# Attention on one Trainium2 core: the eleven phases of a unit get a table of their own

## The chip, the cores and the metric

The kernel runs on one core of one Trainium2 chip. The metric is device time in microseconds (us) of one execution. A profiled execution of the same program gives the start and the duration of every instruction; its own time stands in the table below.

## The reference

Four layers follow each other on one sequence of S = 2048 tokens with D = 576 features. Layers 0 and 2 are attention with H = 32 heads of Dh = 18 features ("A"); layers 1 and 3 have 32 query heads and one head of keys and values ("B").

```python
x = x + _A_ref(_layernorm(x), A_wqkv, A_wo)
x = x + _B_ref(_layernorm(x), B_wq, B_wk, B_wv, B_wo)
x = x + _A_ref(_layernorm(x), A_wqkv, A_wo)
x = x + _B_ref(_layernorm(x), B_wq, B_wk, B_wv, B_wo)
# in each _ref, per head:
scores = einsum("bhqd,bhkd->bhqk", q, k) * Dh ** -0.5
o = einsum("bhqk,bhkd->bhqd", softmax(scores), v)      # then all heads @ wo
```

All is in float32.

## The kernel before

**Units.** Two heads form a pair p; four blocks u of 512 queries form the sequence. One (p, u) is a unit: 64 units in a layer, 256 in the program. A row vector of q or k is held in three parts (54 rows) with a few more rows for the maximum; head a = 0 lies in partitions 0 to 63, head a = 1 in partitions 64 to 127. So a row product uses one half of the TensorE array, and two of them, one on each half, can run side by side.

**What a unit does.** The scores are computed twice. The first time, for the maximum over the keys: 32 row products of 62 rows and 512 columns (`max_mm`, L506, "m" below). Two of them fill the two banks of a tile `psm`, and one VectorE reduction (L515) takes both, so a unit has 16 reductions. There are two `psm` tiles, so the third pair can begin when the first has been reduced. After the last pair of a unit `max_final` (L625) reduces the 32 partial maxima to 8 columns of negated maxima, two small GpSimd operations split them, VectorE transposes them (L634), and DMAs put them into two rows of q. The maxima run 28 pairs, that is 1.75 units, ahead of the rest. The second time, the maximum is subtracted in the product itself: 32 row products of 64 rows and 512 columns (`exp_mm`, L649, "e" below), each into one of three banks `pse`, each followed by a ScalarE exponential (L653) into an SBUF tile `pt`. Then the value products (`pv_block`, L674): four `pt` tiles at a time are multiplied with the values, on four column groups of 32 columns of the array side by side, and accumulated in the one bank `oacc`; ones beside the values give the sums of the softmax. A block has 512 columns, a unit eight blocks, 4096 columns. At the end of a unit ScalarE copies `oacc` (L680), and GpSimd and DMAs do the division.

**The order of the work.** Every engine works through its instructions in the order of the program. The loop over `phase` writes that order out: eleven phases make a unit, numbered 0 to 10 here. A phase is a run of row products, followed by a number of value columns, two phases behind. Before the change `ORDERS` has three kinds of phase: even phases (0, 2, 4, 6, 8) have five row products, odd ones seven, and phase 10 has four. In all phases the halves alternate. With two rows of different halves side by side a phase of five takes three slots of time, one of seven takes four, and phase 10 two: 5 x 3 + 5 x 4 + 2 = 37 slots, of which ten hold a single row, each the last of its phase. A phase has 384 value columns, phase 10 has 256. The maxima's heads are the `n ^ k // 2 % 2` of the loop. `run_todo` issues the small steps and DMAs of finished units at the beginning of the phases, by the number of exponentials issued so far.

The rest of a layer (projections, layer norm, the output projection) is not touched.

Of the kernel before, what the change touches and what calls it, by code (L numbers as in the profile page):

```python
# [19 lines left out]
NCH = S // P  # L20
NPAIR = H // 2
# [21 lines left out]
STEPS = 8  # L43
LEAD = 14
# [14 lines left out]

ORDERS = ([("m", 1), ("e", 0), ("m", 1), ("e", 1), ("e", 2)],
          [("m", 0), ("m", 1), ("e", 1), ("e", 0), ("m", 0), ("m", 1), ("e", 2)],
          [("m", 1), ("e", 0), ("m", 1), ("e", 1)])


@with_exitstack
def tile_kernel(ctx: ExitStack, tc: tile.TileContext, A_x, A_wqkv, A_wo, B_x, B_wq, B_wk, B_wv, B_wo, out):
# [53 lines left out]
    def mtile2(name):  # L123
        return psum.tile([P, 2, 512], F32, tag="m", bufs=2, name=name)
# [7 lines left out]
    def ptile(name, shape=(P, 512), dt=F32):  # L132
        return pool.tile(list(shape), dt, tag="p", bufs=15, name=name)
# [200 lines left out]
    def out_proj(last):  # L334

        for c in range(NCH):
            tt = c // 2
            if c == 1:
                out_rows(2)
            if c % 2 and tt + 3 < 8:  # L340
                out_rows(tt + 3)
            if c >= OUT_AHEAD:
                run_tail(TAIL)
            out_w(c)
            if c % 2 == 0 and tt + 1 < 8:
                out_t(tt + 1, nc.scalar)
            if last:
                nc.sync.dma_start(y_out[c * P:(c + 1) * P, :], xo[:, c])
            yield c
        assert not tail and not ors  # L350
# [4 lines left out]
    for layer in range(4):  # L355
# [124 lines left out]
        def ops(p):  # L480
            return big[:, q_slot(p)], big[:, k_slot(p)]

        m_open, m_next, m_done, m_count = [], [0, 0], [0], {}

        m_first = [] if is_a else ([(0, i // 2, i % 2) for i in range(8)] + [(1, i // 2, i % 2) for i in range(4)] +
                                   [(0, i, 2) for i in range(4)] + [(1, i // 2, i % 2) for i in range(4, 6)] +
                                   [(0, i, 3) for i in range(4)] + [(1, i // 2, i % 2) for i in range(6, 8)] +
                                   [(1, i, 2) for i in range(4)] + [(1, i, 3) for i in range(4)])

        def max_mm(a, slot):  # L490

            i = m_next[a]
            p, u = divmod(i // 16, 4)
            if i < len(m_first):
                u, qc, kb = m_first[i]
            else:
                qc, kb = i // 2 % 4, i // 8 % 2 * 2 + i % 2
            q, k = ops(p)
            if (p, u) not in mxs:
                mxs[p, u] = pool.tile([P, 32], F32, name="mx")  # L500
            if m_done[0] % 2 == 0:
                m_open.append((mtile2("psm"), []))
            ps, rows = m_open[0]
            b = 64 * a
            c0 = u * 512 + qc * P
            nc.tensor.matmul(ps[:, slot], q[b:b + KM, c0:c0 + P], k[b:b + KM, kb * 512:(kb + 1) * 512],  # L506
                             start=True, stop=True)
            rows.append((p, u, 16 * a + 4 * qc + kb))
            m_next[a] += 1
            m_done[0] += 1  # L510
            if m_done[0] % 2 == 0:
                m_open.pop()
                (p, u, r0), (p1, u1, r1) = sorted(rows)
                assert (p, u) == (p1, u1)
                nc.vector.reduce_max(mxs[p, u][:, r0:r1 + 1:r1 - r0], ps, axis=AX.X)  # L515
                m_count[p, u] = m_count.get((p, u), 0) + 2
                if m_count[p, u] == 32:
                    max_final(p, u)

        def max_pair():  # L520
            if is_a and m_done[0] % 4 == 0:
                run_todo(m_done[0] // 4)
            for a in range(2):
                max_mm(a, a)
            if not is_a and m_done[0] == 46:
                max_store(0, 0)
            elif not is_a and m_done[0] == 54:
                max_rows(0, 0)
# [94 lines left out]
        def max_final(p, u):  # L623
            neg = pool.tile([P, 8], F32, name="neg")
            nc.vector.tensor_reduce(neg, mxs.pop((p, u)).rearrange("p (b k) -> p b k", k=4), axis=AX.X, op=OP.max,  # L625
                                    negate=True)
            hl = nms[p, u] = hls[(4 * p + u) % 2]
            copy(nc.gpsimd, hl[:, 0:8], neg)
            nc.gpsimd.tensor_tensor(hl[:, 8:16], neg, hl.bitcast(F32)[:, 0:8], op=OP.subtract)

        def max_store(p, u):

            tr = pool.tile([P, 32], F32, name="tr")
            nc.vector.transpose(tr, nms.pop((p, u)).bitcast(F32))  # L634
            for b in range(4):
                nc.sync.dma_start(m_d[u].rearrange("j a q (b i) -> b (j a q) i", b=4)[b], tr[32 * b:32 * b + 16, :])

        def max_rows(p, u):
            for a in range(2):
                nc.sync.dma_start(big_f[64 * a + KM:64 * a + KE, q_slot(p), u * 512:(u + 1) * 512],  # L640
                                  m_d[u][:, a].rearrange("j q p -> j (q p)"))

        def exp_mm(p, u, i, tail):

            a, kc = (i // 2) % 2, i // 4 * 2 + i % 2
            q, k = ops(p)
            e = (mtile if tail and i % 2 else etile)("pse")
            r = 64 * a
            nc.tensor.matmul(e, k[r:r + KE, kc * P:(kc + 1) * P], q[r:r + KE, u * 512:(u + 1) * 512],  # L649
                             start=True, stop=True)  # L650

            pt = pts[p, u, i] = ptile("pt")
            nc.scalar.activation(pt, e, AF.Exp, scale=SCALE)  # L653
# [3 lines left out]
        def pv_cols(cols):  # L657

            while cols:
                n, c0 = divmod(pv_at[0], 512)  # L660
                w = min(cols, 512 - c0)
                pv_block(n, c0, c0 + w)
                pv_at[0] += w
                cols -= w

        def pv_block(n, c0, c1):

            p, u, i = *divmod(n // STEPS, 4), n % STEPS * 4
            cs = slice(c0, c1)
            turn[0] += 1  # L670
            for i in range(i, i + 4) if turn[0] % 2 else range(i + 3, i - 1, -1):
                a, kc = (i // 2) % 2, i // 4 * 2 + i % 2
                j = 64 * a + 32 * (kc % 2)
                nc.tensor.matmul(oacc[j:j + DH + 1, cs], v_of(kc)[:, 2 * p + a if is_a else 0, :], pts[p, u, i][:, cs],  # L674
                                 start=kc < 2 and c0 == 0, stop=kc >= 14 and c1 == 512)
                if c1 == 512:
                    pts.pop((p, u, i))
            if c1 == 512 and i // 4 == STEPS - 1:
                oc = ocs[p, u] = ptile("oc")
                nc.scalar.activation(oc, oacc, AF.Copy)  # L680
# [38 lines left out]
        def at(b, f, *args):  # L719
            todo.setdefault(b, []).append((f, args))  # L720

        ns = STEPS * 4 * NPAIR
        for p in range(NPAIR):
            for u in range(4):
                b = STEPS * (4 * p + u) + STEPS - 1
# [20 lines left out]
        def run_todo(st):  # L746
            for n in sorted(n for n in todo if n <= st):
                for f, args in todo.pop(n):
                    f(*args)
# [4 lines left out]
        at(b - 1, out_rows, 1)  # L754
        left = 2 * LEAD - m_done[0] // 2
        woven(max_pair, left, len(fill) * len(TERMS) // left)
        for f, args in fill:
            f(*args)
        assert not weave["left"]
        exps = 0  # L760
        for phase in range(11 * 4 * NPAIR):
            k = phase % 11
            run_todo(LEAD + exps // 4)
            for kind, n in ORDERS[2 if k == 10 else k % 2]:
                if kind == "e":
                    n += exps
                    exp_mm(*divmod(n // 4 // STEPS, 4), n % (4 * STEPS), m_done[0] >= 4 * ns)
                elif m_done[0] < 4 * ns:
                    max_mm(n ^ k // 2 % 2, m_done[0] % 2 if k % 2 == 0 else n ^ k // 2 % 2)
            exps += 2 if k == 10 else 3  # L770
            if phase >= 2:
                pv_cols(256 if k == 10 else 384)
        outs = out_proj(layer == 3)
        for st in range(ns, ns + L_AT + 1):
            run_todo(LEAD + st)
            if st < ns + OUT_AHEAD:
                next(outs)
                pv_cols(256 * (1 + st - ns))
        tail = [todo.pop(n, []) for n in range(ns + LEAD + L_AT + 1, ns + LEAD + O_AT)]
        assert not todo, todo  # L780

# [30 lines left out]
```

## Time and profile before

| | |
|---|---|
| median of 3 runs | 5818.13 us (5813.65 to 5818.87) |
| profiled execution, its own time | 5815.04 us |
| its span, first to last instruction | 5813.3 us |
| TensorE matmuls, busy | 5783.1 us (99%) |
| VectorE, busy | 5173.7 us (89%) |
| ScalarE, busy | 4604.9 us (79%) |
| GpSimd, busy | 1714.7 us (29%) |
| row products for the exponentials (L649) | 8192, 2450.5 us |
| row products for the maxima (L506) | 8192, 2296.7 us |
| granted TensorE clock | 0.998 |

In the profile PE is TensorE's matmuls and PEld its weight loads, DVE is VectorE, ACT ScalarE, POOL GpSimd, SP the engine that issues the DMAs. Busy times are sums over overlapping work: a busy PE is not a PE at its peak, since matmuls of two halves or of four column groups run at once. A line of a timeline has the start, the time to the end of the last merged instruction, the engine, line and tile, the number of merged instructions, and in brackets the idle time before it and what ended it.

### The profile page before, as it was taken

The page shows a single profiled execution, that of the slowest core. Times are in us where ns is not written, and L with a number is a line of the kernel's source. Part 1 is how long each engine was busy: PE and PEld are TensorE (multiplying, and loading weights), DVE is VectorE, ACT ScalarE, POOL GpSimd, SP SyncE. Part 2 cuts the span into 40 slices and gives each one's busy share as a digit, 9 for nine tenths or more (in the row PEclk, how much of TensorE's full clock was granted, in tenths as well). Part 3 has the DMA queues.
Part 4 walks back from the last instruction along what each step waited for, and adds up shares of the span by engine and source line. Part 5 has one row for each costly group of instructions (what it writes and reads, how often), then busy time and mean ns, then how long its engine had stood idle before and what let it go on. Part 6 is the DMA issues. An engine that isn't in the chain of part 4 may idle for free.

```text
span 5813.3 us, 132695 instructions
## 1 busy us (share of the span) xinstructions
PE 5783.1 (99%) x53756; PEld 2903.9 (50%) x53756; DVE 5173.7 (89%) x5336; ACT 4604.9 (79%) x8872; POOL 1714.7 (29%) x2207
## 2 busy tenths in 40 slices
PE   9999999999999999999999999999999999999999
PEld 7644444444844444444685444444448444444446
DVE  4799999998699999999637999999976999999995
ACT  2588888888378888888625888888882888888885
POOL 2132322223233232323311323232342332323232
PEclk9999999999999999999999999999999999999999
DMA  5311111110320000000243111111114100000002
GB/s 199 105 44 32 35 32 34 33 32 22 126 65 23 23 20 22 20 22 23 59 167 89 42 35 31 35 31 35 29 32 129 51 22 23 22 23 19 23 14 77
DMA packets 250305, 276.40 MB, mean 48 GB/s; under 512 B 131732, under 2 KB 171924, under 8 KB 239972
## 3 DMA queue, kind: packets, MB, share of 16 engines
q1 hardware_dynamic: 249692, 267.92, 16.6%
q8 instruction: 422, 6.91, 0.5%
q14 instruction: 191, 1.56, 0.1%
HBM read 151.24 MB, written 112.56 MB: 45 GB/s over the span
## 4 chain that ended last, share of the span: by engine, by line
PE 97%; DVE 1%; DMA 0%; POOL 0%; ACT 0%; issue 0%; SPq 0%; POOLq 0%; ACTq 0%; DVEq 0%
PE oacc L674 36%; PE psm L506 31%; PE pse L649 17%; PE psn L215 6%; PE psq L374 6%; DVE mx L515 1%; PE ps L207 0%; DMA raw<-in_B_wk_dram 0%; ACT pt L653 0%; PE oacc L208 0%; SPq L151 0%; POOL big L162 0%; DMA raw<-in_A_wqkv_dram 0%; DVE xh L255 0%; DVE st L244 0%
## 5 line engine op out<-in xcount | busy, mean ns | idle before, releaser
L515 DVE TENSOR_REDUCE mx<-psm 128x2 f32<-128x1024 f32 x4096 | 4771.9, 1217 | 172.8 <-PE psm L506 130.6
L653 ACT ACTIVATE pt<-pse 128x512 f32<-128x512 f32 x8192 | 4315.4, 603 | 543.7 <-PE pse L649 376.3
L649 PE MATMUL pse<-big 64*128 64x512 f32 x8192 | 2450.5, 417 | 3.1 <-ACT evr L385 1.8
L506 PE MATMUL psm<-big 62*128 62x512 f32 x8192 | 2296.7, 453 | 6.8 <-DVE mx L515 6.5
L674 PE MATMUL oacc<-pt,vbuf 128*19 128x384 f32 (+1 forms) x24560 | 1757.1, 385 | 1.9 <-ACT oc L680 1.9
L506 PEld LDWEIGHTS psm<-big 62*128 62x128 f32 x8192 | 926.5, 184 | 1480.1 <-DVE mx L515 926.9
L649 PEld LDWEIGHTS pse<-big 64*128 64x128 f32 x8192 | 1188.6, 185 | 286.4 <-ACT pt L653 192.8
L674 PEld LDWEIGHTS oacc<-pt,vbuf 128*19 128x19 f32 x24560 | 500.9, 97 | 773.2 <-issue 595.7
L139 POOL TENSOR_SCALAR hl<-neg 128x8 fp32r<-128x8 f32 x256 | 50.6, 198 | 2669.7 <-DVE neg L625 2669.7
L674 PE MATMUL oacc<-pt,vy 128*19 128x256 f32 x8176 | 592.0, 384 | 0.0
L697 POOL TENSOR_TENSOR rl<-lt,mone 128x8 f32<-128x8 f32 x256 | 422.5, 1651 | 572.2 <-DMA lt<-os 572.1
L139 POOL TENSOR_SCALAR os<-oc 32x512 f32<-32x512 f32 x512 | 313.3, 612 | 130.8 <-ACT oc L680 88.7
L710 POOL TENSOR_TENSOR os<-os,rb 96x512 f32<-96x512 f32 x256 | 328.3, 1282 | 21.1 <-DMA rb<-r_d 20.3
L688 POOL TENSOR_TENSOR os<-os,oc 96x512 f32<-96x512 f32 x256 | 326.2, 1274 | 21.3
L382 ACT ACTIVATE ev<-psq 128x512 fp32r<-128x512 f32 (+1 forms) x112 | 66.9, 597 | 329.2 <-PE psq L374 229.9
L215 PE MATMUL psn<-wsm,xx 128*128 128x288 f32 x2240 | 313.3, 297 | 0.0
L215 PEld LDWEIGHTS psn<-wsm,xx 128*128 128x128 f32 x2240 | 299.3, 188 | 15.9 <-issue 15.6
L674 PEld LDWEIGHTS oacc<-pt,vy 128*19 128x19 f32 x8176 | 177.0, 98 | 249.6 <-issue 200.6
L388 DVE TENSOR_TENSOR ev<-psq,ev 128x512 fp32r<-128x512 f32 (+1 forms) x84 | 58.0, 690 | 217.4 <-ACT ev L382 201.7
L374 PE MATMUL psq<-yx,big 128*128 128x512 f32 (+2 forms) x812 | 200.2, 397 | 2.1 <-ACT big L137 0.8
L374 PE MATMUL psq<-xx,big 128*128 128x512 f32 (+1 forms) x784 | 201.0, 401 | 0.0
L680 ACT ACTIVATE oc<-oacc 128x512 f32<-128x512 f32 x256 | 158.2, 618 | 28.2 <-PE oacc L674 28.2
(66 smaller groups left out, 1367.2 us busy)
## 6 DMA issues: line engine op xcount, KB each, us to landing
big<-qk_d SPq DMA_DIRECT2D x180, 432.0 KB
qk_d<-ev SPq DMA_DIRECT2D x96, 512.0 KB
qk_d<-ev SPq DMA_DIRECT2D x120, 256.0 KB
rb<-r_d SPq DMA_DIRECT2D x512, 36.0 KB
o_d<-os SPq DMA_DIRECT2D x512, 36.0 KB
m_d<-tr SPq DMA_DIRECT2D x1024, 2.0 KB
o<-o_d SPq DMA_DIRECT2D x64, 256.0 KB
big<-m_d SPq DMA_DIRECT2D x512, 4.0 KB
```

What stands on the lines that cost most here:

```text
L139: eng.tensor_scalar(dst, src, 1.0, 0.0, op0=OP.mult, op1=OP.add)
L215: nc.tensor.matmul(ps, lhs[:, xc, :], wsm[:, wc, h * 288:(h + 1) * 288], start=i == 0, stop=i == len(TERMS) - 1)
L374: nc.tensor.matmul(ps[:n].rearrange("p (u t) -> p u t", u=2)[:, us], w[:, wc, :n], xts[T][:, us, xc, :], start=j == 0, stop=j == len(TERMS ...
L506: nc.tensor.matmul(ps[:, slot], q[b:b + KM, c0:c0 + P], k[b:b + KM, kb * 512:(kb + 1) * 512], start=True, stop=True)
L515: nc.vector.reduce_max(mxs[p, u][:, r0:r1 + 1:r1 - r0], ps, axis=AX.X)
L649: nc.tensor.matmul(e, k[r:r + KE, kc * P:(kc + 1) * P], q[r:r + KE, u * 512:(u + 1) * 512], start=True, stop=True)
L653: nc.scalar.activation(pt, e, AF.Exp, scale=SCALE)
L674: nc.tensor.matmul(oacc[j:j + DH + 1, cs], v_of(kc)[:, 2 * p + a if is_a else 0, :], pts[p, u, i][:, cs], start=kc < 2 and c0 == 0, stop=k ...
L680: nc.scalar.activation(oc, oacc, AF.Copy)
L688: nc.gpsimd.tensor_tensor(t[:96], t[:96], oc[:96], op=OP.add)
L697: nc.gpsimd.tensor_tensor(rl, lts.pop((p, u)), mone, op=OP.pow)
L710: nc.gpsimd.tensor_tensor(t[:96], t[:96], rb[:96], op=OP.mult)
```

## The change

Each of the eleven phases gets an entry of its own in a table: the order of its row products (m or e, with the head) and its number of value columns. The exponentials are now taken head by head (`e_next`), the maxima in the order of the table; `m_heads` lists the heads of all maxima in advance, and `m_banks` tells for each pair which of the two goes to which bank of `psm`, so that the reduction's output can be written in rising order.

```diff
-ORDERS = ([("m", 1), ("e", 0), ("m", 1), ("e", 1), ("e", 2)],
-          [("m", 0), ("m", 1), ("e", 1), ("e", 0), ("m", 0), ("m", 1), ("e", 2)],
-          [("m", 1), ("e", 0), ("m", 1), ("e", 1)])
+UNIT = [("m1 m0 e0 e0 e1 m0 m1", 352), ("e1 m0 e1 m1 e0", 384), ("m0 m1 e1 e1 e0 m1 m0", 384), ("e0 m1 m0 e0 e1", 384),
+        ("m1 e0 e1 m0 e0 m1", 352), ("m0 e1 e0 m1 e1 m0", 416), ("e0 e1 m0 m0 e1", 192), ("e0 m1 e1 m0", 320),
+        ("m0 m1 e0 e0 e1 m0 m1", 384), ("e1 e0 m1 m1 e0", 352), ("m0 m1 e1 e1 e0 m1 m0", 576)]
+UNIT = [([(o[0], int(o[1])) for o in rows.split()], cols) for rows, cols in UNIT]
...
-        def max_mm(a, slot):
+        def max_place(a, i):
...
+        m_heads = ([0, 1] * (2 * LEAD) + [g for rows, _ in UNIT for kind, g in rows if kind == "m"] * (4 * NPAIR))[:4 * ns]
+        m_banks, n = [], [0, 0]
+        for i in range(0, 4 * ns, 2):
+            at_ = []
+            for a in m_heads[i:i + 2]:
+                p, u, qc, kb = max_place(a, n[a])
+                at_.append((p, u, 16 * a + 4 * qc + kb))
+                n[a] += 1
+            m_banks += [0, 1] if at_[0] < at_[1] else [1, 0]
+
+        def max_mm():
+
+            a, slot = m_heads[m_done[0]], m_banks[m_done[0]]
+            p, u, qc, kb = max_place(a, m_next[a])
...
-        exps = 0
-        for phase in range(11 * 4 * NPAIR):
-            k = phase % 11
-            run_todo(LEAD + exps // 4)
-            for kind, n in ORDERS[2 if k == 10 else k % 2]:
+        e_next = [0, 0]
+        for phase in range(len(UNIT) * 4 * NPAIR):
+            rows, cols = UNIT[phase % len(UNIT)]
+            run_todo(LEAD + sum(e_next) // 4)
+            for kind, a in rows:
                 if kind == "e":
-                    n += exps
-                    exp_mm(*divmod(n // 4 // STEPS, 4), n % (4 * STEPS), m_done[0] >= 4 * ns)
+                    pu, kc = divmod(e_next[a], NCH)
+                    exp_mm(*divmod(pu, 4), kc // 2 * 4 + 2 * a + kc % 2, m_done[0] >= 4 * ns)
+                    e_next[a] += 1
                 elif m_done[0] < 4 * ns:
-                    max_mm(n ^ k // 2 % 2, m_done[0] % 2 if k % 2 == 0 else n ^ k // 2 % 2)
-            exps += 2 if k == 10 else 3
+                    max_mm()
             if phase >= 2:
-                pv_cols(256 if k == 10 else 384)
+                pv_cols(cols)
...
-                pv_cols(256 * (1 + st - ns))
+                pv_cols(512 if st > ns else UNIT[0][1] + UNIT[1][1] - 512)
```

Per unit there are still 32 row products of each kind, 4096 value columns in eleven runs, and 16 stretches of columns into which the block boundaries cut them. Phases 0, 2, 8 and 10 now have seven rows, 1, 3, 6 and 9 five, 4 and 5 six, and phase 7 four.

More of the change, by code (lines that the diff above doesn't have):

```diff
@@ L488, in tile_kernel @@
                                    [(1, i, 2) for i in range(4)] + [(1, i, 3) for i in range(4)])
-        def max_mm(a, slot):
-            i = m_next[a]
+        def max_place(a, i):
             p, u = divmod(i // 16, 4)
             if i < len(m_first):
-                u, qc, kb = m_first[i]
-            else:
-                qc, kb = i // 2 % 4, i // 8 % 2 * 2 + i % 2
+                return (0, *m_first[i])
+            return p, u, i // 2 % 4, i // 8 % 2 * 2 + i % 2
+        ns = STEPS * 4 * NPAIR
+        m_heads = ([0, 1] * (2 * LEAD) + [g for rows, _ in UNIT for kind, g in rows if kind == "m"] * (4 * NPAIR))[:4 * ns]
[10 more added lines that the diff above has]
+            p, u, qc, kb = max_place(a, m_next[a])
             q, k = ops(p)
@@ L522, in max_pair @@
                 run_todo(m_done[0] // 4)
-            for a in range(2):
-                max_mm(a, a)
+            max_mm()
+            max_mm()
             if not is_a and m_done[0] == 46:
@@ L720, in at @@
             todo.setdefault(b, []).append((f, args))
-        ns = STEPS * 4 * NPAIR
         for p in range(NPAIR):
@@ L759, in tile_kernel @@
         assert not weave["left"]
-        exps = 0
-        for phase in range(11 * 4 * NPAIR):
-            k = phase % 11
-            run_todo(LEAD + exps // 4)
-            for kind, n in ORDERS[2 if k == 10 else k % 2]:
+        e_next = [0, 0]
[3 more added lines that the diff above has]
+            for kind, a in rows:
                 if kind == "e":
-                    n += exps
-                    exp_mm(*divmod(n // 4 // STEPS, 4), n % (4 * STEPS), m_done[0] >= 4 * ns)
+                    pu, kc = divmod(e_next[a], NCH)
+                    exp_mm(*divmod(pu, 4), kc // 2 * 4 + 2 * a + kc % 2, m_done[0] >= 4 * ns)
+                    e_next[a] += 1
                 elif m_done[0] < 4 * ns:
-                    max_mm(n ^ k // 2 % 2, m_done[0] % 2 if k % 2 == 0 else n ^ k // 2 % 2)
-            exps += 2 if k == 10 else 3
+                    max_mm()
             if phase >= 2:
-                pv_cols(256 if k == 10 else 384)
+                pv_cols(cols)
         outs = out_proj(layer == 3)
```

## The prediction

> **What bounds the kernel now.** The first thing read is the page's list of engines and its costliest groups, the second the list of waits.
>
> ```profile
> PE 5783.1 (99%) x53756; PEld 2903.9 (50%) x53756; DVE 5173.7 (89%) x5336; ACT 4604.9 (79%) x8872; POOL 1714.7 (29%) x2207
> L515 DVE TENSOR_REDUCE mx<-psm 128x2 f32<-128x1024 f32 x4096 | 4771.9, 1217 | 172.8 <-PE psm L506 130.6
> L680 ACT ACTIVATE oc<-oacc 128x512 f32<-128x512 f32 x256 | 158.2, 618 | 28.2 <-PE oacc L674 28.2
> PEld psm L506 <- DVE mx L515: 926.9, 2021, 2.8
> PEld pse L649 <- ACT pt L653: 192.8, 995, 0.4
> ```
>
> PE is occupied all the time, but DVE is close behind, and the weight loads of both kinds of row products wait for the engine that empties their banks. Much of that waiting hides under matmuls already running, so the timeline has to say what a unit costs. Its period is the distance of two copies of `oacc`:
>
> ```profile
> 712.05 0.62 ACT L680 ACTIVATE oc<-oacc 128x512 f32<-128x512 f32 x1
> 731.41 0.62 ACT L680 ACTIVATE oc<-oacc 128x512 f32<-128x512 f32 x1
> ```
>
> 19.36 us. The maxima run 28 pairs ahead, which is 1.75 of 64 units; so 62.25 units of a layer, 249 of the program, have both kinds of rows and this period. 0.01 us in it is 2.5 us of the program.
>
> Next PE's own timeline, phases 10 (two slots of row products), 1 (four) and the beginning of 2 (three):
>
> ```profile
> 726.29 0.50 PE L506 MATMUL psm<-big 62*128 62x512 f32 x1
> 726.63 0.39 PE L506 MATMUL psm<-big 62*128 62x512 f32 x1
> 726.95 0.63 PE L674 MATMUL oacc<-pt,vy 128*19 128x256 f32 x8
> 727.51 0.50 PE L506 MATMUL psm<-big 62*128 62x512 f32 x1
> ...
> 729.20 0.51 PE L506 MATMUL psm<-big 62*128 62x512 f32 x2
> 729.54 0.43 PE L649 MATMUL pse<-big 64*128 64x512 f32 x2
> 729.77 0.42 PE L506 MATMUL psm<-big 62*128 62x512 f32 x2
> 730.00 0.39 PE L649 MATMUL pse<-big 64*128 64x512 f32 x1
> 730.32 0.84 PE L674 MATMUL oacc<-pt,vy 128*19 128x384 f32 x8
> 731.09 0.50 PE L506 MATMUL psm<-big 62*128 62x512 f32 x1
> ...
> 732.09 0.52 PE L674 MATMUL oacc<-pt,vbuf 128*19 128x384 f32 x4
> ```
>
> Counted from a phase's start, the slots begin at 0, 0.34, 0.57 and 0.80; the value products follow 0.32 after the last. So the rows take 0.66 with two slots (measured), 1.13 with four (1.12 here; 1.13 to 1.14 in the neighbours), and 0.57 + 0.33 = 0.90 with three. Value columns: 0.77 for 384, 0.56 for 256, so 0.13 for the run and 0.00167 per column. A slot that holds one row is as long as one with two: 730.00 to 730.32 against 726.63 to 726.95.
>
> Before, without waits: 5 x 1.13 + 5 x 0.90 + 0.66 = 10.81 for rows and 10 x 0.77 + 0.56 = 8.26 for values, 19.07 in all. Of the 0.29 up to 19.36 one sees 0.10 in phase 2 (731.09 to 732.09 is 1.00, not 0.90: the copy of `oacc` is late), 0.11 in phase 5 and 0.02 each in some phases of three slots. Here are phases 4 and 5:
>
> ```profile
> 734.77 0.49 PE L649 MATMUL pse<-big 64*128 64x512 f32 x1
> 735.25 0.18 PEld L649 LDWEIGHTS pse<-big 64*128 64x128 f32 x1 [0.19 <-ACT pt L653]
> 735.33 0.60 ACT L653 ACTIVATE pt<-pse 128x512 f32<-128x512 f32 x1
> 735.68 0.85 PE L674 MATMUL oacc<-pt,vbuf 128*19 128x256 f32 x16
> 736.46 0.50 PE L506 MATMUL psm<-big 62*128 62x512 f32 x2
> 737.03 0.19 PEld L506 LDWEIGHTS psm<-big 62*128 62x128 f32 x2 [0.28 <-DVE mx L515]
> 737.37 0.40 PE L649 MATMUL pse<-big 64*128 64x512 f32 x1
> 737.70 0.84 PE L674 MATMUL oacc<-pt,vbuf 128*19 128x384 f32 x8
> ```
>
> The load of 737.03 waited for a reduction. The next slot is 0.34 behind it, as behind the first slot of a phase (731.09 is followed by 731.43), not 0.23; so after a late load the row streams 0.11 later than the load starts, and that is paid on top. The same at 735.25: the values follow 0.43 behind the load, 0.11 + 0.32. Now the two engines that release the banks:
>
> ```profile
> 729.74 3.49 DVE L515 TENSOR_REDUCE mx<-psm 128x2 f32<-128x1024 f32 x3 [0.21 <-PE psm L506]
> 733.26 0.19 DVE L625 TENSOR_REDUCE neg<-mx 128x8 f32<-128x32 f32 x1
> 733.40 2.36 DVE L515 TENSOR_REDUCE mx<-psm 128x2 f32<-128x1024 f32 x2
> 735.67 0.20 DVE L634 STREAM_TRANSPOSE tr<-hl 128x32 f32<-128x32 f32 x1
> 729.97 1.58 ACT L653 ACTIVATE pt<-pse 128x512 f32<-128x512 f32 x3 [0.32 <-PE pse L649]
> 731.60 0.18 PEld L649 LDWEIGHTS pse<-big 64*128 64x128 f32 x1 [0.21 <-ACT pt L653]
> ```
>
> A pair in slot 1 (729.20) is reduced from 0.54 on. Reductions in a row start (3.49 - 1.22) / 2 = 1.14 apart, and a bank comes free 1.22 after the start. Around the small reduction of a finished unit the distance is longer: the third of the first group starts at 729.74 + 3.49 - 1.22 = 732.01, the next at 733.40, 1.39 later. An exponential starts 0.43 behind a row in slot 2 (729.54 to 729.97) and 0.56 behind one in slot 1 (734.77 to 735.33). Three in a row end 1.58 after the first starts, two 1.09 (1.58 less half of 1.58 - 0.60). A load follows a release by 0.05 (729.97 + 1.58 = 731.55, load 731.60).
>
> **The change part by part.**
>
> *Slots.* Row by row the table makes 4, 3, 4, 3, 3, 3, 3, 2, 4, 3, 4 slots: 36. Rows without waits: 4 x 1.13 + 6 x 0.90 + 0.66 = 10.58, 0.23 less than before, 57 us in 249 units. The Trainium skill, "TensorE: Matmul & The Clock Gate", section "Back-to-back issue gap", has 216 ns for 512 columns; by it the slot would be worth an estimated 54 us, and the trace's 0.23 stands.
>
> Ten single rows were last in their phase; eight now stand in mid-phase, with the next row on the same half (e0, e0). Only the last 1.75 units of a layer have such a place before:
>
> ```profile
> 1438.37 0.74 PE L649 MATMUL pse<-big 64*128 64x512 f32 x3
> 1439.04 0.85 PE L674 MATMUL oacc<-pt,vbuf 128*19 128x256 f32 x16
> ```
>
> These are e0, e0, e1: 0.67 to the values, as much as two full slots (0.66). So I take no surcharge. Its bound above is a load that is not hidden, 0.11 per place; below, nothing is gained, as the place is still a slot.
>
> *Value columns.* Still 4096 in eleven runs: 8.26. The period without waits is 18.84.
>
> *The copy of `oacc`.* It starts behind phase 1's three exponentials, which start 0.56 into that phase, 0.97 + 0.48 later at 2.01, and ends at 2.63; phase 1 lasts 0.90 + 0.77. The values of phase 2 come 1.13 into that phase, at 2.80. This wait of 0.10 goes.
>
> *Waits for reductions.* A unit's maxima end with the first pair of phase 2. From that phase's start: reduction at 0.54 (the one before, of phase 1, has DVE free at 0.4), then 1.39 to 1.93, which is the second pair of phase 2, then 1.14 to 3.07, the pair of phase 3. Its banks are free at 4.29, and the load that needs them starts at 4.34 and streams at 4.45. That row is the last m1 of phase 4, in slot 3, which without waits streams at 1.90 + 1.67 + 0.57 = 4.14. **Wait (a): 0.31.** The values of phase 4 queue behind it on PE, so nothing covers it; the pair's other half comes in phase 5, and DVE idles for 0.5. The other pairs are 1.1 to 1.4 apart and find their banks free by 0.0 to 0.5.
>
> *Waits for exponentials.* An e needs the bank of the third e before it.
> - **(b)** Phase 6 has two e in slot 1 and few columns, 0.90 + 0.45 = 1.35. Its second exponential ends at 0.56 + 1.09 = 1.65, the load is at 1.70, 0.35 into phase 7, and streams at 0.46 instead of 0.34: 0.12. The m0 behind it waits too.
> - **(c)** Phase 9 starts with two e and lasts 0.90 + 0.72. Its third exponential ends at 0.56 + 1.58 = 2.14; load at 2.19, 0.57 into phase 10, streaming at 0.68 instead of 0.57: 0.11, passed on by the m0 on the same half.
> - **(d)** Phase 0 lasts 1.13 + 0.72; its exponentials start at 0.34 + 0.43 = 0.77 and end at 2.35; load at 2.40, 0.55 into phase 1, streaming at 0.66 instead of 0.57: 0.09.
>
> The e of phases 3 and 4 that come 0.03 late lie under (a); one in phase 9 shortens (c) by as much.
>
> *Sum.* 18.84 + 0.31 + 0.12 + 0.11 + 0.09 = 19.47 against 19.36: 0.11 longer, 27 us in 249 units. The slot is won and more than lost again. The profiled execution took 5815.04 us, so 5842 in its terms; the median is 3 us above it, so 5845. Tails of layers, bound by exponentials, and all DMAs stay as they are, being hung on the number of exponentials, which runs alike to phase 6.
>
> **The rivals.**
>
> *Loads go ahead of the waits (faster).* If only the row product waited for its bank and its load were already done, each of (a) to (d) would lose 0.11: 0.20 + 0.01 + 0 + 0 leaves 19.05, 0.31 below 19.36, 77 us: 5741. It decides wherever a load can overtake a release. Against it: in the rows above the load itself stands behind the wait (735.25, 737.03). The Trainium skill, "TensorE: Matmul & The Clock Gate", section "Step-by-step: what each phase is for", says that loads can be pulled ahead of running matmuls. By that rule this rival would win; the trace agrees with it only for loads without a wait. Chance 0.08.
>
> *ScalarE is a little earlier (faster).* If exponentials started 0.1 sooner than 0.56 and 0.77, (b), (c) and (d) would be gone: 19.15, 52 us, 5766. As DVE would then be pressed sooner, half is likelier: 5792. The waits are margins of 0.1 in a chain of 2, which speaks for it. Chance 0.16.
>
> *Evens out.* The wait (a) rests on the pair of phase 2 arriving no earlier than DVE; with 0.2 instead of 0.31 the period is 19.36 again: 5818. Chance 0.13.
>
> *Single rows in mid-phase are dearer (slower still).* Six of the eight places lie outside the stretch of (a). At 0.03 each that adds 45 us, 5890, at the full 0.11 another 164 us, 6009. Against it speaks the tail's 0.67. Chance 0.13.
>
> *The table does not give 36 slots* would need two neighbouring rows of different halves not side by side; rows 729.20 and 729.54 with x2 show pairs of both kinds. Counted in the last rival.
>
> **How the numbers follow.** The forecast itself, 5830 to 5865, has 0.50. Slower: 0.50 + 0.13 = 0.63; same 0.13; faster 0.16 + 0.08 = 0.24. About 0.2%, 12 us, is what can be told from no change. The range of 8 in 10 takes in the partial gains and the small surcharge, 5775 to 5890, and leaves out the first rival and most of the last.
>
> **What would show it.** Period of the copies 19.47; PEld idle before phase 4's last load with DVE as releaser; DVE idle 0.5 before a pair split over phases 4 and 5; late e loads in phases 7, 10 and 1; values of phase 2 no longer behind the copy. A period under 19.3 makes the prediction wrong, and which of the four loads is on time says by which step.

## The result

The changed kernel takes 5842.88 us, median of 6 runs (5837.93 to 5846.04), against 5817.65 us (5813.65 to 5818.87) of the kernel before: ratio 1.0044, 95% interval 1.0031 to 1.0057. It is 25 us slower; 5845 was forecast, in a range of 5775 to 5890. Its profiled execution took 5844.74 us, 29.7 more than the one before, with a span of 5842.9 us.

### The profile page after: what moved, and what is told of

Same layout as the page of the kernel before. It is cut to its first block, busy times and chain, and to the rows that moved or that the text cites. A ratio compares the mean times of both kernels' runs of the same rounds, so it can differ in the third digit from the quotient of the medians.

```text
span 5842.9 us, 132674 instructions
## 1 busy us (share of the span) xinstructions
PE 5807.1 (99%) x53756; PEld 3143.3 (54%) x53756; DVE 5209.0 (89%) x5336; ACT 4585.4 (78%) x8872; POOL 1715.9 (29%) x2207
## 4 chain that ended last, share of the span: by engine, by line
PE 97%; DVE 1%; POOL 0%; ACT 0%; DMA 0%; issue 0%; SPq 0%; POOLq 0%; ACTq 0%; DVEq 0%
PE oacc L689 36%; PE pse L664 26%; PE psm L521 22%; PE psn L215 6%; PE psq L374 6%; DVE mx L530 1%; PE ps L207 0%; ACT pt L668 0%; DMA raw<-in_B_wk_dram 0%; PE oacc L208 0%; DVE xh L255 0%; DMA raw<-in_A_wqkv_dram 0%; DVE st L244 0%; POOL big L162 0%; SPq L153 0%
## 5 line engine op out<-in xcount | busy, mean ns | idle before, releaser
L521 PE MATMUL psm<-big 62*128 62x512 f32 x8192 | 2504.1, 451 | 5.2 <-DVE mx L530 4.9
L664 PE MATMUL pse<-big 64*128 64x512 f32 x8192 | 2381.3, 449 | 9.6 <-DMA big<-m_d 6.5
L664 PEld LDWEIGHTS pse<-big 64*128 64x128 f32 x8192 | 1231.4, 185 | 812.8 <-ACT pt L668 678.8
L521 PEld LDWEIGHTS psm<-big 62*128 62x128 f32 x8192 | 1084.8, 184 | 814.0 <-DVE mx L530 555.6
L689 PE MATMUL oacc<-pt,vy 128*19 128x384 f32 (+1 forms) x8176 | 569.8, 385 | 0.0
```

## The profile after

The page's list of engines, the costliest group on DVE, and the two lines of the list of waits that answer to those of before (line, who waited for whom: us in all, times, longest):

```profile
PE 5807.1 (99%) x53756; PEld 3143.3 (54%) x53756; DVE 5209.0 (89%) x5336; ACT 4585.4 (78%) x8872; POOL 1715.9 (29%) x2207
L530 DVE TENSOR_REDUCE mx<-psm 128x2 f32<-128x1024 f32 x4096 | 4797.3, 1221 | 160.3 <-PE pse L664 71.8
PEld pse L664 <- ACT pt L668: 678.8, 1508, 0.9
PEld psm L521 <- DVE mx L530: 555.6, 1241, 2.4
```

Every count is the same, and no busy share moved by more than a point or two, save PEld's. What moved is who is waited for: loads of the exponentials' rows now wait 679 us for ScalarE instead of 193. The waits for reductions fell from 927 to 556 us, yet the kernel is slower: most of the idle time of a load lay under running matmuls before, and the sum of a waits line doesn't tell how much did not. (Of the 1120 us of both lines before, the table below shows 0.25 a unit as waits of any kind, 11.06 less 10.81, some 62 us in 249 units.) The period tells it, in ACT's timeline:

```profile
716.08 0.62 ACT L695 ACTIVATE oc<-oacc 128x512 f32<-128x512 f32 x1
735.54 0.62 ACT L695 ACTIVATE oc<-oacc 128x512 f32<-128x512 f32 x1
```

The period is 19.46 us here and 19.43 as the median, against 19.36. The distance from a phase's first row product to its first value product, the median over the units of the profiled executions, shows where (no-wait values: 0.66 with two slots, 0.90 with three, 1.13 with four):

| phase | 0 | 1 | 2 | 3 | 4 | 5 | 6 | 7 | 8 | 9 | 10 | sum |
|---|---|---|---|---|---|---|---|---|---|---|---|---|
| before | 0.91 | 1.13 | 0.99 | 1.13 | 0.92 | 1.24 | 0.89 | 1.13 | 0.92 | 1.14 | 0.66 | 11.06 |
| after | 1.13 | 0.97 | 1.13 | 0.92 | 1.12 | 0.90 | 0.90 | 0.75 | 1.18 | 0.90 | 1.20 | 11.12 |
| after, without waits | 1.13 | 0.90 | 1.13 | 0.90 | 0.90 | 0.90 | 0.90 | 0.66 | 1.13 | 0.90 | 1.13 | 10.58 |

The value runs take 8.30 in both. So the rows needed 0.23 less and got 0.54 of waits, 0.29 more than before. The largest is in phase 4. Here are lines from phase 2 on, picked out of PE's, DVE's and PEld's timelines:

```profile
715.84 0.51 PE L521 MATMUL psm<-big 62*128 62x512 f32 x2
713.93 3.69 DVE L530 TENSOR_REDUCE mx<-psm 128x2 f32<-128x1024 f32 x3
717.65 0.18 DVE L640 TENSOR_REDUCE neg<-mx 128x8 f32<-128x32 f32 x1
717.75 2.35 DVE L530 TENSOR_REDUCE mx<-psm 128x2 f32<-128x1024 f32 x2
719.46 0.50 PE L521 MATMUL psm<-big 62*128 62x512 f32 x1
...
719.92 0.18 PEld L664 LDWEIGHTS pse<-big 64*128 64x128 f32 x1 [0.17 <-ACT pt L668]
720.02 0.20 DVE L649 STREAM_TRANSPOSE tr<-hl 128x32 f32<-128x32 f32 x1
720.15 0.18 PEld L521 LDWEIGHTS psm<-big 62*128 62x128 f32 x1
720.27 1.23 DVE L530 TENSOR_REDUCE mx<-psm 128x2 f32<-128x1024 f32 x1
720.58 0.79 PE L689 MATMUL oacc<-pt,vbuf 128*19 128x256 f32 x16
...
721.84 4.67 DVE L530 TENSOR_REDUCE mx<-psm 128x2 f32<-128x1024 f32 x4 [0.35 <-PE pse L664]
```

The third reduction of the first group starts at 713.93 + 3.69 - 1.22 = 716.40, 0.56 into phase 2; behind the small reduction come two more, which end at 717.75 + 2.35 = 720.10; the load of phase 4's last m1 follows at 720.15, and the values 0.43 behind it, 1.12 into the phase. No bracket marks this wait: the load of the e beside it, itself late, ends at 720.10, so the loader idles for 0.05 only. It is read from the start alone, and the experiments below test it. The pair of phase 4's first two m is reduced at 720.27; then DVE idles for 0.35, until the split pair's other half, in phase 5, has come.

Phases 7 and 8 in the same unit:

```profile
724.39 0.50 PE L664 MATMUL pse<-big 64*128 64x512 f32 x1
724.72 0.18 PEld L664 LDWEIGHTS pse<-big 64*128 64x128 f32 x1
725.15 0.73 PE L689 MATMUL oacc<-pt,vbuf 128*19 128x320 f32 x8
725.82 0.50 PE L521 MATMUL psm<-big 62*128 62x512 f32 x2
726.57 0.18 PEld L521 LDWEIGHTS psm<-big 62*128 62x128 f32 x2 [0.20 <-DVE mx L530]
727.00 0.84 PE L689 MATMUL oacc<-pt,vy 128*19 128x384 f32 x8
```

In phase 7 the second load starts 0.33 into the phase, and the values follow 0.43 later. In phase 8 the second pair waits 0.05 for the reduction of phase 7's pair. That is the last of the four from 721.84 on, which start (4.67 - 1.22) / 3 = 1.15 apart, against 1.13 in a row without a pause; so the late m0 of phase 7 can have cost this reduction no more than about 0.05, and VectorE is pressed there in any case.

## The experiments

All ratios are to the kernel before, run beside (medians 5819.23 to 5822.25 us).

**Reliefs: is it the waits, and what is the slot worth?** Four kernels, in which the exponentials, the reductions or both are made shorter. The shorter reductions leave out half of the keys; the shorter exponentials leave out 96 of the 512 columns of a tile. The value products then read each `pt` from its first column on, so that they stay as long as they were (8.30 a unit in all four).

```diff
-            nc.scalar.activation(pt, e, AF.Exp, scale=SCALE)
+            nc.scalar.activation(pt[:, :416], e[:, :416], AF.Exp, scale=SCALE)
...
-            cs = slice(c0, c1)
+            w = min(c1 - c0, 416)
+            cs = slice(c0, c0 + w)
...
-                nc.vector.reduce_max(mxs[p, u][:, r0:r1 + 1:r1 - r0], ps, axis=AX.X)
+                nc.vector.reduce_max(mxs[p, u][:, r0:r1 + 1:r1 - r0], ps[:, :, :256], axis=AX.X)
```

Exponentials alone:

> The changed kernel with exponentials of 416 instead of 512 columns; the value products read what there is, so 96 of 512 columns are left out of the softmax's numerator and sum. Every exponential frees its bank about 0.08 us sooner, three in a row 0.24 sooner. My theory (late exponentials cost the waits (b), (c), (d), which the trace after shows as 0.09 in phase 7, 0.05 in phase 8, 0.07 in phase 10, 0.07 in phase 1): these go, up to 0.28 a unit, 70 us; part may return as a wait for reductions: 5770 to 5800. Rival 1 (the reductions alone hold the changed kernel back): unchanged, 5843 within 10. Rival 2 (a single row in mid-phase costs more than a slot): unchanged too, with the rows of phases 1, 7 and 10 still long.

Measured: 5792.43 us, 0.9957 (0.9942 to 0.9972). Phases 1, 7 and 10 fall to 0.90, 0.67 and 1.13 (medians), all of (b) to (d); phase 4 keeps its wait (1.15), and phase 8 rises from 1.18 to 1.23. So phase 8's wait for a reduction does not go with the late m0 of phase 7; with that phase shorter, it grows.

Reductions alone:

> The changed kernel with reductions over 256 of the 512 columns of each bank: half of the keys are left out of the maximum. A reduction takes about 0.6 us less, VectorE is no longer near full. My theory (wait (a), the last m1 of phase 4, waits for the chain of reductions behind the unit's end): phase 4 loses its 0.22, 55 us: 5780 to 5800; the waits for exponentials stay. Rival 1 (the wait in phase 4 is not VectorE's): 5843.

Measured: 5792.73 us, 0.9957 (0.9942 to 0.9972). Phase 4 falls from 1.12 to 0.91, phases 1, 7 and 10 keep their waits (0.97, 0.76, 1.18), phase 5 rises from 0.90 to 0.99.

Both, in the changed kernel and in the one before:

> The changed kernel with both reliefs, 416 columns of each exponential and 256 of each bank in the reductions. If all that stands between 36 slots and their gain are the waits for banks, the period is the sum without waits, 18.84 to 18.88: 0.55 less than measured, 136 us, and some more from the ends of layers, which are bound by exponentials: 5690 to 5710. Rival (single rows in mid-phase are dearer, 0.03 to 0.11 each at eight places): 0.24 to 0.88 above that, over 5750.

> The kernel before with the same two reliefs. Without waits its period is 19.07 to 19.11, 0.25 under the measured 19.36: 62 us less, some more from the ends of layers: 5745 to 5765. Its distance from the changed kernel with both reliefs is the worth of the slot alone: 0.23 a unit, 57 us, if a slot is a slot wherever it stands; nothing or less than nothing if single rows in mid-phase are dearer.

Measured: 5697.12 us, 0.9792 (0.9775 to 0.9808), and 5747.36 us, 0.9879 (0.9865 to 0.9894). Two copies of `oacc` in each, the changed kernel's first:

```profile
700.38 0.60 ACT L696 ACTIVATE oc<-oacc 128x512 f32<-128x512 f32 x1
719.28 0.60 ACT L696 ACTIVATE oc<-oacc 128x512 f32<-128x512 f32 x1
```

```profile
706.68 0.60 ACT L681 ACTIVATE oc<-oacc 128x512 f32<-128x512 f32 x1
725.80 0.60 ACT L681 ACTIVATE oc<-oacc 128x512 f32<-128x512 f32 x1
```

The periods are 18.90 and 19.12. In both kernels the rows of all phases are at their no-wait values (medians; 10.59 and 10.81 in sum), and the slot is worth 0.22 a unit; the two times are 50 us apart. The change does what it says, and single rows in mid-phase cost no more than a slot; that rival falls. The reliefs take 146 us from the changed kernel and 72 from the one before. Of these 134 and 62 are the period's (0.54 and 0.25 in 249 units); the rest is mostly at the beginnings and ends of the layers. The two reliefs alone gave 50 us each, together 146: each kind of wait hides part of the other.

**The small reduction at a unit's end.** Without it the chain to phase 4 is shorter at one link only.

```diff
-            nc.vector.tensor_reduce(neg, mxs.pop((p, u)).rearrange("p (b k) -> p b k", k=4), axis=AX.X, op=OP.max,
-                                    negate=True)
+            mx4 = mxs.pop((p, u)).rearrange("p (b k) -> p b k", k=4)
+            nc.gpsimd.tensor_scalar(neg, mx4[:, :, 0], -1.0, 0.0, op0=OP.mult, op1=OP.add)
```

> The changed kernel without the small VectorE reduction at a unit's end: GpSimd takes the first of the four partial maxima of each query and negates it, so three quarters of the keys are left out of the maximum. My theory: the chain behind phase 2's first pair is 1.14 instead of 1.39, so the last m1 of phase 4 finds its bank 0.25 sooner and phase 4 loses its 0.22, 55 us, of which up to half comes back one phase later, as phase 5 lengthened by 0.09 when the reductions were halved: 5785 to 5815. Rival (what delays phase 4 is how full VectorE is as a whole, 16 reductions a unit, not this one reduction at this place): 0.25 of 18.5 less, at most a few us where it binds: 5835 to 5843.

Measured: 5835.61 us, 1.0027 (1.0017 to 1.0037), a miss by 20 us at least, and a time at which the rival had put it. But phase 4 loses its whole wait, which speaks against the rival's mechanism. The theory's mechanism is there, and its gain is not. PE's, PEld's and DVE's timelines, phases 4 and 5:

```profile
719.31 0.50 PE L521 MATMUL psm<-big 62*128 62x512 f32 x1
719.65 0.64 PE L521 MATMUL psm<-big 62*128 62x512 f32 x2
720.11 3.72 DVE L530 TENSOR_REDUCE mx<-psm 128x2 f32<-128x1024 f32 x3 [0.26 <-PE psm L521]
720.22 0.79 PE L689 MATMUL oacc<-pt,vbuf 128*19 128x256 f32 x16
720.94 0.49 PE L521 MATMUL psm<-big 62*128 62x512 f32 x1
721.39 0.18 PEld L521 LDWEIGHTS psm<-big 62*128 62x128 f32 x1 [0.16 <-DVE mx L530]
722.05 0.90 PE L689 MATMUL oacc<-pt,vbuf 128*19 128x416 f32 x8
```

Phase 4 takes 0.91 as expected. But phase 5 now comes 0.22 sooner, its second m needs the bank of phase 4's first pair, and that pair is reduced no sooner, since its reduction waits for its row, 0.80 into phase 4 as before (720.11 here, 720.27 above). So the load waits until 0.45 into phase 5, which takes 1.11 instead of 0.90. The wait moved by one phase with 0.21 of its 0.22, and the period is 19.42 instead of 19.43. I had allowed for half. The 7 us by which the time lies below the changed kernel's are 2 or 3 by the period; the rest was not taken apart.

**One row moved: what did the 36th slot buy?**

```diff
-        ("m1 e0 e1 m0 e0 m1", 352), ("m0 e1 e0 m1 e1 m0", 416), ...
+        ("m1 e0 e1 m0 e0", 352), ("m1 m0 e1 e0 m1 e1 m0", 416), ...
```

> The changed kernel with one row moved over one run of value columns: the last m1 of phase 4 becomes the first row of phase 5, which then has seven rows and four slots. All work is done, in 37 slots again. My theory (the slot that the two phases of six rows save is spent at the bank of that m1): phase 4 loses its wait of 0.22, phase 5 gains a slot of 0.23, and the period stays within 0.05: 5830 to 5855. Rival (a slot is worth its 0.23 also here): 57 us slower, 5895 to 5905.

Measured: 5841.08 us, 1.0037 (1.0024 to 1.0050), the same as the changed kernel. PE's timeline, phases 4 and 5:

```profile
698.57 0.50 PE L521 MATMUL psm<-big 62*128 62x512 f32 x1
699.48 0.79 PE L689 MATMUL oacc<-pt,vbuf 128*19 128x256 f32 x16
700.20 0.50 PE L521 MATMUL psm<-big 62*128 62x512 f32 x2
701.34 0.89 PE L689 MATMUL oacc<-pt,vbuf 128*19 128x416 f32 x8
```

The rows take 0.91 and 1.14, without a wait in either, in place of 1.12 and 0.90. So with 37 slots the period is 19.43 as with 36: the saved slot had been spent at the bank of one m1.

**Orders and columns.** Tables that all do the whole work; a line that begins with "..." has the columns alone. First the changed kernel's orders with even columns:

```diff
-... 352 384 384 384 352 416 192 320 384 352 576
+... 384 384 384 384 384 384 384 256 384 384 384
```

> The table's row orders with even value columns: 384 in every phase, 256 in the short phase 7. The waits (b), (c) and (d) have more time, up to 0.2 a unit less. But phases 10 and 0, with four pairs of maxima in a row, 4 x 1.14 = 4.56 of VectorE, get 1.90 + 1.90 instead of 2.30 + 1.86, 0.36 less. My theory (banks of the maxima bind as much as those of the exponentials, and the columns are what spaces them): 0.05 to 0.25 a unit slower, 5855 to 5905. Rival (the uneven columns are the harm, because short phases wait for exponentials): 0.1 to 0.2 faster, 5795 to 5820.

Measured: 5901.68 us, 1.0142 (1.0127 to 1.0157). PE's timeline, a phase 0:

```profile
718.83 0.50 PE L521 MATMUL psm<-big 62*128 62x512 f32 x2
719.17 0.64 PE L664 MATMUL pse<-big 64*128 64x512 f32 x3
719.86 0.50 PE L521 MATMUL psm<-big 62*128 62x512 f32 x2
720.29 0.85 PE L689 MATMUL oacc<-pt,vy 128*19 128x256 f32 x16
```

The second pair starts 1.03 into the phase instead of 0.81, and the values come at 1.46: four pairs in two phases come faster than they are reduced.

Then the orders of the kernel before, written as rows of the table, with the change's columns:

```diff
+UNIT = [("m1 e0 m1 e0 e1", 352), ("m0 m1 e0 e1 m0 m1 e0", 384), ("m0 e1 m0 e1 e0", 384), ("m1 m0 e1 e0 m1 m0 e1", 384),
...
+        ("m1 e0 m1 e0 e1", 384), ("m0 m1 e0 e1 m0 m1 e0", 352), ("m0 e1 m0 e1", 576)]
```

> The row orders of before (37 slots) with the value columns of the table. My theory: orders and columns belong together. The old orders have a pair of maxima in slots 1 and 3 of a phase of seven; between phase 5 and phase 7 there are five pairs, 5.7 us of VectorE, and phases 5 to 7 last 1.95 + 1.35 + 1.80 = 5.1 instead of 5.6, so the reductions hold phases 6 to 8 back by 0.2 to 0.4 a unit, of which the wide phase 10 gives nothing back: 5865 to 5920. Rival (the columns are good or bad by themselves, as even ones cost the table's orders 0.27): the old orders gain from them too or stay, 5760 to 5820.

Measured: 5880.26 us, 1.0105 (1.0090 to 1.0120): phases 5 and 7 take 1.30 and 1.36 (medians) instead of 1.24 and 1.13. Neither half of the change helps by itself: with even columns the new orders lose another 59 us, and the old orders lose 61 us by the change's columns.

And the change's orders with other columns:

```diff
-... 352 384 384 384 352 416 192 320 384 352 576
+... 352 384 512 320 320 384 256 320 384 352 512
```

> The table's row orders with other columns: 352, 384, 512, 320, 320, 384, 256, 320, 384, 352, 512. Phases 2 and 3 together are 0.11 longer, so the chain of reductions from phase 2 to phase 4 costs 0.11 less of waiting; phase 6 is 0.11 longer, so the second exponential of phase 6 is no longer late for phase 7 (0.09, and 0.05 in phase 8). No work is left out. My theory: 0.10 to 0.20 a unit less, 5795 to 5820. Rival (a wait that goes comes back elsewhere, since each bank is needed again two pairs or three exponentials later): 5835 to 5850.

Measured: 5832.08 us, 1.0021 (1.0012 to 1.0031), 11 us better than the change and a miss: phase 7 falls to 0.71 and phase 1 to 0.91, but phase 4 keeps 1.05, phase 5 rises to 1.03 and phase 0 to 1.19 (medians). This is the rival's mechanism, though not its number.

Two tables with other orders, the second also with a later use of the maxima's banks by the exponentials:

```diff
+UNIT = [("e1 m0 e0 m1 e1", 384), ("m1 m0 e0 m0 e1 m1 e0", 448), ("e0 m0 m1 e1 e0", 352), ("m1 m0 e1 e1 m0 e0 m1", 384),
+        ("m1 e0 m1 e0 e1", 384), ("m1 m0 e0 e1 e1 m0 m1", 352), ("e0 m1 e1 m0", 288), ("m1 e0 m0 e1 e1", 320),
+        ("e0 m1 m0 e1 m0 m0 e1", 320), ("e0 m1 e0 m0 e1", 448), ("m1 m0 e0 e1 e0 m1 m0", 416)]
```

```diff
+UNIT = [("m1 m0 e0 m0 e1 m1 e0", 384), ("e0 m1 e0 e1 m0", 384), ("m0 m1 e1 e0 e1 m1 m0", 384), ("m1 e0 m0 e1 e1", 416),
+        ("m1 m0 e1 e1 e0 m1 m0", 384), ("e0 m1 e1 m0 e0", 384), ("m0 m1 e0 e0 e1 m0 m1", 384), ("m0 e1 m1 e0 e0", 384),
+        ("m0 m1 e1 e0 e1 m1 m0", 352), ("e1 m0 m1 e0", 256), ("m1 m0 e1 e0 e1", 384)]
```

> Another table with all the work: the orders begin phases with rows of both kinds, spread the maxima over the phases and spare the e that need the bank of a late exponential; 37 slots, one more than the change, as many as before. My theory (what counts is the sum of slots and waits): 0.23 more for the slot, but the waits, 0.54 a unit in the changed kernel, shrink to 0.1 to 0.25: period 19.1 to 19.3, 5750 to 5800, faster than both kernels. Rival (the number of slots decides): not faster than the changed kernel, 5843 or more.

> A second table with all the work: nearly even columns (256 in a phase of four rows, 352 and 416 once each, 384 otherwise), phases of seven and five rows in turn as before the change, 37 slots, but with the second pair of a phase of seven in its last slot instead of its third, 0.24 later, so that its bank has been reduced, and the late e ahead of it. Also the exponentials of the phase in which the maxima end do not yet use the maxima's banks, which should take the 0.75 us by which a layer's end became longer. My theory: the slots stay, phase 5's wait of 0.11 and phase 2's 0.10 of before go: period 19.15 to 19.25, 5765 to 5800. Rival (36 slots are needed for a gain): 5815 or more.

Measured: 5799.01 us, 0.9964 (0.9951 to 0.9977), and 5812.38 us, 0.9988 (0.9978 to 0.9997). The first is faster than both kernels, with 37 slots and a period of 19.24 (median): its rows take 10.93 in all, so that only 0.12 of waits are left, against 0.54 with the change's 36 slots. The second missed its 5800 by 12 us, with 19.31; its rows take 11.00, that is 0.19 of waits, most of it in three phases that take 0.04 to 0.05 too long each.

**The ends of the layers.** The trace after shows the last two units of a layer 1.3 us longer than before in three layers (40.8 against 39.5) and 1.0 in the other. The prediction had this at nothing.

```diff
             rows, cols = UNIT[phase % len(UNIT)]
+            late = m_done[0] >= 4 * ns
...
-                    exp_mm(*divmod(pu, 4), kc // 2 * 4 + 2 * a + kc % 2, m_done[0] >= 4 * ns)
+                    exp_mm(*divmod(pu, 4), kc // 2 * 4 + 2 * a + kc % 2, late)
```

> The changed kernel in which the exponentials of the phase where a layer's maxima end do not yet use the maxima's banks. In the trace after, that phase (m m e e e) lasts 3.00 us instead of 2.25 before, its e waiting for reductions. My theory: these two e wait for the last two reductions, so the phase falls below 2.0 and a layer's last two units take about 1 us less, 4 us in all, 5836 to 5842, to be read in the trace rather than in the time. Rival (the longer ends come from the uneven columns, since a phase of 192 or 320 columns is shorter than its three exponentials): the phase gets shorter, but the last two units stay at 40.8 us a layer.

Measured: 5834.89 us, 1.0023 (1.0014 to 1.0033), 8 us below the changed kernel and 1 below the range. The phase where a layer's maxima end, PE's timelines of the kernel before, the changed one and this one:

```profile
1434.68 0.50 PE L506 MATMUL psm<-big 62*128 62x512 f32 x1
1435.73 0.50 PE L649 MATMUL pse<-big 64*128 64x512 f32 x2 [0.31 <-DVE mx L515]
1436.16 0.84 PE L674 MATMUL oacc<-pt,vbuf 128*19 128x384 f32 x8
```

```profile
1443.11 0.50 PE L521 MATMUL psm<-big 62*128 62x512 f32 x2
1444.91 0.50 PE L664 MATMUL pse<-big 64*128 64x512 f32 x1 [0.51 <-ACT pt L668]
1445.34 0.84 PE L689 MATMUL oacc<-pt,vbuf 128*19 128x384 f32 x8
```

```profile
1440.90 0.49 PE L521 MATMUL psm<-big 62*128 62x512 f32 x2
1441.23 0.63 PE L664 MATMUL pse<-big 64*128 64x512 f32 x3
1441.82 0.84 PE L689 MATMUL oacc<-pt,vbuf 128*19 128x384 f32 x8
```

The rows take 1.48, 2.23 and 0.92. The bracket names ScalarE, but the wait went away with the other choice of bank. The bank that was no longer chosen is one that a reduction empties, and the last reduction ended just then, beside an exponential.

The last two units take 39.5 us in every layer again, so the rival's 40.8 falls. But that doesn't put all of the 1.3 us on this phase. The phase was late before the change too, by less (1.48 against 0.92): the change made it 0.75 longer. The very last unit of a layer takes 23.07 in this kernel as in the changed one, against 22.6 before (22.9 in one layer). This half microsecond stays, hidden in the 39.5 by the shorter phase, and what it comes from was not tested; the uneven columns are not ruled out for it.

So the trace shows 5 us less in the four layers' ends. What else the time fell by is not at this place: between the two profiled executions, 9.5 us apart, it lies mostly in the first units of the layers and in one long unit, which the edit doesn't touch.

## Why the prediction was right, and where it was off

*The slot.* 0.23 was taken; the two kernels with both reliefs are 0.22 apart. There is no surcharge for single rows in mid-phase: phase 0 takes 1.13 and phase 9 0.90, the no-wait values.

*The copy of `oacc`.* Phase 2's wait of 0.10 went, as forecast: 1.13.

*Wait (a).* Forecast 0.31, measured 0.22. Mechanism and place were right, and DVE idles behind it as forecast, for 0.35 and not 0.5. The size was off. In the unit shown, phases 2 and 3 took 0.05 longer than in the sum (an e of phase 3 is late), and the bank came free 0.03 sooner (the reductions start 1.35 and 1.13 apart instead of 1.39 and 1.14, the first of them 0.02 later). Both leave less to wait for.

*Waits (b) to (d).* Forecast 0.12, 0.11 and 0.09; measured 0.09, 0.07 and 0.07, each 0.02 to 0.04 too high. What was missed: 0.05 in phase 8, a wait for a reduction, where I had the pairs finding their banks free "by 0.0 to 0.5", a margin too thin to be called free.

*Sum.* The waits came to 0.54 instead of 0.63, the value runs to 0.04 more in both kernels; the period grew by 0.07 and not 0.11. In the profiled executions the units but for a layer's first and last two are 19 us longer in all (27 forecast), the last two of the layers 5 (nothing forecast), the first units 3, and the stretches before a layer's first exponential row 3, which the change doesn't touch. (Of the first units' 3, 2.7 fall in one layer, and the trace of the last experiment doesn't have them there.) So the 25 us of the medians are near the forecast partly because two errors cancel: a steady term too large and a missing one at the layers' ends. "Tails of layers, bound by exponentials, and all DMAs stay as they are" was, for the tails, the step that failed: it took them as bound by exponentials and left out the phase in which the maxima end, 0.75 of the 1.3 us; the 0.5 in the last unit stays open.

*The rivals.* Loads do not go ahead of a wait: in phase 4 the load itself starts 0.05 behind the end of the reduction (720.15 and 720.10), and where the late load shown is a phase's last, the values are 0.43 behind it. The Trainium skill, "TensorE: Matmul & The Clock Gate", section "Step-by-step: what each phase is for", lets loads be pulled ahead of running matmuls; here none of those shown passed a wait for a bank. "ScalarE is a little earlier" has its mechanism shown by the shorter exponentials (50 us), but without them it did not happen. "Evens out" got near with the wait (a), 0.22 against its 0.2, but the period still grew by 0.07.

*What stays open.* The two other tables show that faster orders exist; which banks the second one's remaining waits are for was not taken apart, nor was the last unit of a layer.

## What to carry to other kernels

A slot removed from the fullest engine is worth its time only if the buffers behind it are free sooner too. Here three engines pass banks in a ring, two deep for the maxima and three for the exponentials, and a slot saved was waited out at the next bank. Walk one period row by row, with the release time of every buffer, before counting slots; where a removed wait leads, look one phase on, and look at the ends of the loop, where the banks change hands.

## What the runs showed of the hardware

A row product whose load starts late costs more than the lateness: the next slot follows 0.34 us behind that load, not 0.23 (737.03 to 737.37 in the kernel before), and the values 0.43, not 0.32 (720.15 to 720.58). That is 0.11 on top. VectorE's reductions last 1.22 us but start 1.13 apart in a row. The small reduction, which reads what the last one has written, starts only when that one has ended (717.65, 1.25 behind it), while the transpose, which reads other data, starts 1.14 behind (720.02). With the small reduction between them, two reductions start 1.35 to 1.39 apart. Exponentials last 0.60 and start 0.48 apart. So the mean durations in the list of groups overstate these two engines, and a dependent step costs more than its own duration says.
